# Zero products early on TensorE, half-line offsets for the project operands, and a GpSimd way for weight parts: a float32 attention and MLP kernel on one core

## The chip, the cores and the metric

The kernel runs on one core of a Trainium2 chip. The metric is the device time of one execution in microseconds (us). Engines carry the names of the profile: PE is TensorE (PEld its weight loads), DVE is VectorE, ACT is ScalarE, POOL is GpSimd and SP is SyncE; a q behind a name (PEldq, SPq) marks the engine's instruction queue.

## What is computed

Local attention with a few global keys, and two gated MLPs behind it, all in float32, for 2 batches of 768 positions. Cut to what matters:

```python
scores = scale * q @ k.T + bias            # 8 heads of 64; kept: 96 back, 8 global keys
a = softmax(scores); x = a @ v             # (2, 768, 512)
gate = sigmoid(causal_conv5(x, conv_w))    # first MLP, d_model 512
x = (gate * (x @ w_val)) @ w_out
h = relu(x @ w_in)                         # second MLP, d_ff 1024
out = (h * sigmoid(conv3(h, conv_w2))) @ w_out2
```

The kernel multiplies `w_out` and `w_in` into one matrix W of 512 x 1024 beforehand.

## The kernel before

The 12 tiles of 128 positions (6 per batch) go through attention one by one (`fast_attention`). For each tile PE forms the scores of two halves of 4 heads (L461), DVE adds the bias and takes the row's least value (L472), ACT takes exp and the row sum (L477), DVE inverts the sum and scales (L491, L498), PE transposes (L522), ACT copies the result out of PSUM (L526), and PE multiplies by v (L540). Tile 0 needs only its own keys, which lie in a corner of `x` (`c.first`); every other tile uses its own keys and those of the tile before.

Beside attention the weights are prepared. They arrive as 64-bit numbers in `raw` tiles (`unit`, L291) and become float32 in four steps (`to_f32`): ACT scales (L262), POOL prepares the remainder (L264), DVE joins the bits (L269, L272). The products of the MLPs take each operand as a rounded part (high) and a remainder (low), and `mm3` (L243 to L245) adds three products: high by high, high by low, low by high. `split_ops` makes the two parts: ACT the high (L234), DVE the low (L236). For `w_val` (4 units of 128 x 512, tiles `wvh`, `wvl`) and `w_out2` (8 units, tiles of the pool `w8`), `parts_unit` makes an `m` tile and splits it. W itself is 32 float32 products of 512 columns (L319, `weights`), whose results are split too (`Wh`, `Wl`).

The MLPs run over 4 chunks (2 batches, each of 400 and 368 positions). `values` multiplies by `w_val`, `hidden` by W (operands `gg`), `gated` does the second convolution and gate and splits the result into `g2`, and `project` multiplies `g2` by `w_out2`: for each chunk 3 groups of 128 positions, 8 blocks of 128 of the 1024 columns, 3 products each, 512 columns wide. In the last chunk one group is cut into two of 256. In `project` the parts of `g2` (pool `late`) are what PE loads as weights, and those of `w_out2` (pool `w8`) stream past them. In the profile `g2` and the `w8` tiles are named `g` and `w`, and PSUM tiles `s`, `t`, `x` and `f`.

The order on each engine is made by a planner (class `Plan`). Each piece of work has a list of engines with an assumed cost, its buffers, and what it reads and writes; `lay` goes through time and gives each engine the waiting piece of highest rank, and a piece that has several ways goes to the engine on which it would end first by these costs. So one changed cost or way can move instructions anywhere behind it. Only the first instructions (L834 to L844) stand by hand: the loads of the first tile, the positions, and two loads of a number into a register on every engine (L841), on which a branch depends (L938).

The SBUF pools lie behind each other in the order in which they are opened (`const`, `w8`, `wst`, `sg`, then `at` during attention, whose place `late` takes over). All start at a multiple of 64 bytes.

Of the kernel before, what the change touches and what calls it, by code (L numbers as in the profile page):

```python
# [9 lines left out]
F32 = mybir.dt.float32  # L10
F32R = mybir.dt.float32r
I32 = mybir.dt.int32
AF = mybir.ActivationFunctionType
ALU = mybir.AluOpType
AX = mybir.AxisListType
PSUM = bass.MemoryType.PSUM

P = 128
# [192 lines left out]
def act_us(n, sbuf=True, scaled=False, sums=False):  # L211
    return 0.05 + 0.000834 * n + 0.042 * sbuf + 0.092 * scaled + 0.093 * sums


def dve_us(n, scaled=False):
    return 0.069 + 0.001042 * n + 0.061 * scaled
# [6 lines left out]
def pool_us(n):  # L223
    return 0.17 + 0.0013 * n


def dma_us(kb):
    return max(0.4, kb / 385.0)


def split_ops(c, hi, lo, src, n, bufs, reads, writes, sbuf=True):

    nc, pl = c.nc, c.plan
    pl.add("ACT", act_us(n, sbuf), lambda: nc.scalar.activation(hi(), src(), AF.Copy), bufs, reads, [writes + ("hi",)])  # L234
    pl.add(
        "DVE", dve_us(n), lambda: nc.vector.tensor_tensor(lo(), src(), hi().bitcast(F32), ALU.subtract),  # L236
        bufs, reads + [writes + ("hi",)], [writes + ("lo",)],
    )


# [47 lines left out]
def unit(c, dst, src, a, col, bufs, token, e=None):  # L288

    nc, raw = c.nc, c.raws.new()  # L290
    dma = lambda: nc.sync.dma_start(raw.t.rearrange("p d t -> p (d t)"), rows(src, a, col))  # L291
    c.plan.add("SP", dma_us(512), dma, [raw], [], [("raw", raw)], delay=LANDING)
    view = (lambda: raw.t) if e is None else (lambda: raw.t.rearrange("p (e x) t -> p e x t", e=e))
    to_f32(c, dst, view, 512, [raw] + bufs, [("raw", raw)], token)


def weights(c):
# [35 lines left out]
    for a in range(4):  # L333
        parts_unit(c, c.w_val, a, lambda z, a=a: c.wv[z][:, a, :], [], ("wv", a))


def parts_unit(c, src, a, part, bufs, token):
    m = c.ms.new()
    unit(c, lambda: m.t, src, a, 0, [m], token + ("m",))
    split_ops(c, lambda: part(0), lambda: part(1), lambda: m.t, 512, [m] + bufs, [token + ("m",)], token)  # L340


def second_weights(c):
    c.wo2 = [[c.w8.new() for _ in "hl"] for _ in range(2)]
    for a in range(8):
        two = c.wo2[a // 4]
        parts_unit(c, c.w_out2, a, lambda z, a=a, two=two: two[z].t[:, a % 4, :], two, ("wo2", a))


def scratch(c):  # L350

    x = [c.x[:, d, XP:] for d in range(NC1)]
    c.rel, c.w, c.d = (x[d][:, 0:WIN] for d in range(3))
    c.key, c.far, c.d0 = (x[d][:, 4 * P : 5 * P] for d in range(3))


def positions(c):

    nc = c.nc
    nc.gpsimd.iota(c.rel, pattern=[[-1, WIN]], base=P, channel_multiplier=1, allow_small_or_imprecise_dtypes=True)  # L360
    nc.gpsimd.iota(c.key, pattern=[[1, P]], base=0, channel_multiplier=0, allow_small_or_imprecise_dtypes=True)
    nc.gpsimd.affine_select(
        out=c.rel, in_=c.rel, compare_op=ALU.is_ge, fill=BIG, base=P, pattern=[[-1, WIN]], channel_multiplier=1
    )
# [44 lines left out]
def fast_attention(c, ap):  # L409

    nc, ident, pl = c.nc, c.ident, c.plan
# [9 lines left out]
    kq, vs = {}, {}  # L421

    def keys(t, pr, what):
        return c.first[0][:, pr, what] if t == 0 else kq[t].t[:, pr, what]
# [4 lines left out]
    def load(t):  # L429
        b, i = tiles[t]  # L430
        if t == 0:
            return
        kq[t], vs[t] = kqr.new(), vr.new()
        pl.add("SP", dma_us(512), lambda: nc.sync.dma_start(kq[t].t, c.kq[b, i]), [kq[t]], [], [("kq", t)], delay=LANDING)
        src = c.v[b, i * P : (i + 1) * P].rearrange("s h d -> s (h d)")
        pl.add(
            "SP", dma_us(256), lambda: nc.sync.dma_start(vs[t].t.rearrange("p a h d -> p (a h d)"), src),
            [vs[t]], [], [("v", t)], delay=LANDING,
        )

    def held(d, ts):
        return [d[t] for t in ts if t in d]

    for t in range(nt):
# [3 lines left out]
        js = [t - 1, t] if i else [t]  # L448
        nk = len(js) * P
        st, p = sts.new(), {}  # L450
        load(t)
        for half in range(2):
            s = [c.ring["s"].new() for z in range(2)]

            def scores(half=half, s=s, js=js, t0=t):
                for pr in (2 * half, 2 * half + 1):
                    for n, j in enumerate(js):
                        for z in range(2):
                            hs = slice(z * D, (z + 1) * D)
                            out = s[z].t.rearrange("p (a w) -> p a w", w=WIN)[:, pr % 2, n * P : (n + 1) * P]  # L460
                            nc.tensor.matmul(out, keys(t0, pr, 1)[hs], keys(j, pr, 0)[hs], start=True, stop=True)  # L461

            pl.add(
                "PE", 0.43 * len(js), scores, s + held(kq, js), [("kq", j) for j in js], [("s", t, half)], mode="s"
            )
            for h in range(4 * half, 4 * half + 4):
                p[h] = pr_.new()

                def least(h=h, s=s, st=st, w=p[h], nk=nk, i=i):
                    sc = s[h % 2].t.rearrange("p (a w) -> p a w", w=WIN)[:, h // 2 % 2, :nk]  # L470
                    bias = c.B[:, h, :] if i else c.B0[h]
                    nc.vector.tensor_tensor_reduce(  # L472
                        w.t[:, :nk], sc, bias, -QKSCALE, 3.0e38, ALU.add, ALU.min, st.t[:, 0, h : h + 1]
                    )

                def grow(h=h, st=st, w=p[h], nk=nk):
                    nc.scalar.activation(  # L477
                        w.t[:, :nk], w.t[:, :nk], AF.Exp, bias=st.t[:, 0, h : h + 1], scale=-1.0,
                        accum_out=st.t[:, 1, h : h + 1],
                    )  # L480

                bias = ("B" if i else "B0", h)
                pl.add("DVE", dve_us(nk), least, [p[h], s[h % 2], st], [("s", t, half), bias], [("p", t, h)])
                pl.add("ACT", act_us(nk, True, True, True), grow, [p[h], st], [], [("p", t, h)])
            hs = slice(4 * half, 4 * half + 4)

            def guard(st=st, hs=hs):
                nc.gpsimd.tensor_scalar(st.t[:, 1, hs], st.t[:, 1, hs], 1.0e-9, 1.0, ALU.add, ALU.mult)

            def invert(st=st, hs=hs):  # L490
                nc.vector.reciprocal(st.t[:, 2, hs], st.t[:, 1, hs])  # L491

            four = [("p", t, h) for h in range(4 * half, 4 * half + 4)]
            pl.add("POOL", 0.12, guard, [st], four, [("r", t, half)])
            pl.add("DVE", 0.2, invert, [st], [], [("r", t, half)])
            for h in range(4 * half, 4 * half + 4):
                def on_dve(h=h, st=st, w=p[h], nk=nk):
                    nc.vector.tensor_scalar(w.t[:, :nk], w.t[:, :nk], st.t[:, 2, h : h + 1], None, ALU.mult)  # L498

                pl.add("DVE", 0.13 + 0.00052 * nk, on_dve, [p[h], st], [("r", t, half)], [("p", t, h)])  # L500
# [312 lines left out]
def attention_gated_mlps(ctx, tc, kq, v, nn, w_val, conv_w, w_out, w_in2, w_out2, out):  # L813
    nc = tc.nc
    c = Ctx()
# [4 lines left out]
    c.const = ctx.enter_context(tc.tile_pool(name="const", bufs=1))  # L820
    w8 = ctx.enter_context(tc.tile_pool(name="w8", bufs=1))
    c.wst = ctx.enter_context(tc.tile_pool(name="wst", bufs=1))
    sg = ctx.enter_context(tc.tile_pool(name="sg", bufs=1))
    c.small = ctx.enter_context(tc.tile_pool(name="small", bufs=1, side="right"))
    c.x = c.const.tile([P, NC1, XW], F32, name="x")
# [7 lines left out]
    with tc.manual_schedule():  # L833
        nc.sync.dma_start(c.li.rearrange("p n t -> p (n t)"), c.nn.to_broadcast([P, 4]))  # L834
        nc.scalar.dma_start(k0[:, 0:2], kq[0, 0, :, 0:2])
        nc.sync.dma_start(k0[:, 2:4], kq[0, 0, :, 2:4])
        nc.scalar.dma_start(v0, v[0, 0:P].rearrange("s (a h) d -> s a h d", a=4))
        scratch(c)
        positions(c)
        nc.vector.memset(one, 0.0)  # L840
        _, (glo, ghi, llo, lhi) = nc.values_load_multi_w_load_instructions(c.nn)  # L841
        nc.scalar.activation(one, one, AF.Exp)
        nc.gpsimd.memset(c.x[:, :, 0:XP], 0.0)
        make_identity(nc, c.ident)  # L844
        first_mask(c)
# [9 lines left out]
    def arm(fast):  # L855
        with ExitStack() as es:
# [4 lines left out]
            pl = c.plan = Plan()  # L861
            ap = pools.enter_context(tc.tile_pool(name="at", bufs=1)) if fast else None
            late = {}

            def late_pool():
                if not late:
                    pools.close()
                    late["p"] = pools.enter_context(tc.tile_pool(name="late", bufs=1, reuse_waits="tile"))
                return late["p"]

            def all_keys(b):
# [110 lines left out]
```

## Time and profile before

| | |
|---|---|
| median of 3 runs | 289.07 us (288.51 to 289.23) |
| profiled execution, its own time | 288.96 us |
| its span in the profile | 287.2 us |
| PE busy | 269.2 us, 94% of the span |
| DVE busy | 238.6 us, 83% |
| ACT busy | 192.6 us, 67% |
| POOL busy | 68.5 us, 24% |

The span runs from the first to the last instruction; the rest of the execution's time, 1.8 us, lies around it. Busy time of PE counts overlapping matmuls once, and a matmul is shown longer than the time it keeps the next one waiting, so the distance from one start to the next is what a matmul costs in a row of them.

### The profile page before, as it was taken

The numbers are of one execution on the slowest core, as the hardware profiler recorded it, in microseconds if no ns is written. First come the engines' busy times: TensorE is split into PE (matmuls) and PEld (weight loads), VectorE is DVE, ScalarE is ACT, GpSimd is POOL, SyncE is SP. The second block draws the span as 40 slices with busy tenths as digits, with TensorE's granted clock in tenths as the row PEclk, the third lists the DMA queues.
The fourth block names the chain that finished last, engine by engine and source line by source line (L and its number), as shares of the span: only waits on it lengthen the run. The fifth ranks groups of instructions, "written<-read, shape, count | busy, mean of one in ns | idle before, by whom it ended". The sixth has DMA issues, their size and how long they took to land.

```text
span 287.2 us, 5402 instructions
## 1 busy us (share of the span) xinstructions
PE 269.2 (94%) x1832; PEld 228.0 (79%) x1832; DVE 238.6 (83%) x637; ACT 192.6 (67%) x486; POOL 68.5 (24%) x160
## 2 busy tenths in 40 slices
PE   2687899899999999999999999999999999999993
PEld 2565666565447999999999999988999988899882
DVE  3999999999999999999899999999986654357600
ACT  2899998988568989988778544875355354454510
POOL 4422223522111120212353512360612000003000
PEclk9999999999999999999999999999999999999999
DMA  4984668637406301004510000010000011000112
GB/s 132 362 312 168 188 216 266 237 102 266 149 2 219 102 19 49 10 2 155 181 40 0 2 0 1 1 39 37 38 2 0 0 73 39 37 0 2 40 73 84
DMA packets 10277, 26.18 MB, mean 91 GB/s; under 512 B 1408, under 2 KB 2688, under 8 KB 10240
## 3 DMA queue, kind: packets, MB, share of 16 engines
q1 hardware_dynamic: 9440, 25.22, 26.3%
q10 hardware_dynamic: 800, 0.52, 0.6%
q8 instruction: 16, 0.26, 0.4%
q14 instruction: 21, 0.17, 0.2%
HBM read 22.59 MB, written 3.15 MB: 90 GB/s over the span
## 4 chain that ended last, share of the span: by engine, by line
PE 72%; DVE 20%; issue 3%; DMA 2%; ACT 1%; POOL 1%; SPq 0%; DVEq 0%; POOLq 0%
PE s L244 8%; PE s L245 8%; PE s L243 8%; PE f L243 7%; PE f L245 7%; PE f L244 7%; DVE p L472 5%; DVE p L498 4%; PE s L461 4%; PE x L540 4%; PE t L522 4%; DVE raw L269 3%; PE t L243 2%; PE x L245 2%; PE t L245 2%
## 5 line engine op out<-in xcount | busy, mean ns | idle before, releaser
L652 DVE SCALAR_TENSOR_TENSOR z<-h,cw,z 128x384 f32<-128x384 f32 x64 | 40.6, 643 | 12.6 <-ACT z L647 10.9
L477 ACT ACTIVATE p<-p,st 128x256 f32<-128x256 f32 (+1 forms) x96 | 46.0, 482 | 5.8 <-DVE st L472 5.5
L654 ACT ACTIVATE z<-z 128x384 f32<-128x384 f32 (+2 forms) x48 | 25.0, 523 | 26.7 <-DVE z L652 26.4
L244 PE MATMUL s<-w,g 128*128 128x512 f32 (+1 forms) x104 | 39.2, 377 | 0.0
L245 PE MATMUL s<-w,g 128*128 128x512 f32 (+1 forms) x104 | 39.2, 377 | 0.0
L243 PE MATMUL s<-w,g 128*128 128x512 f32 (+1 forms) x104 | 39.1, 376 | 0.0
L652 DVE SCALAR_TENSOR_TENSOR z<-x,cw,z 128x400 f32<-128x400 f32 (+1 forms) x64 | 38.4, 628 | 0.1
L522 PE MATMUL t<-ident,p 128*128 128x128 f32 x176 | 28.6, 281 | 4.7 <-ACT pts L526 4.7
L498 DVE TENSOR_SCALAR p<-p,st 128x256 f32<-128x256 f32 (+1 forms) x96 | 31.1, 368 | 0.7
L522 PEld LDWEIGHTS t<-ident,p 128*128 128x128 f32 x176 | 19.9, 140 | 14.6 <-ACT pts L526 8.5
L472 DVE CUSTOM_DVE_ANT_0 p<-s,B 128x256 f32<-128x256 f32 x80 | 30.7, 417 | 0.4 <-PE t L522 0.4
L319 PE MATMUL f<-w,w 128*128 128x512 f32 x64 | 30.1, 601 | 0.7 <-DVE Wl L236 0.6
L526 ACT ACTIVATE pts<-t 128x512 f32<-128x512 f32 (+1 forms) x48 | 26.5, 553 | 2.5 <-PE t L522 2.1
L243 PE MATMUL f<-gg,Wh 128*128 128x400 f32 (+1 forms) x80 | 27.7, 346 | 0.0
L245 PE MATMUL f<-gg,Wl 128*128 128x400 f32 (+1 forms) x80 | 27.0, 338 | 0.0
L244 PE MATMUL f<-gg,Wh 128*128 128x400 f32 (+1 forms) x80 | 27.0, 338 | 0.0
L461 PE MATMUL s<-kq 64*128 64x128 f32 x320 | 25.0, 291 | 0.5 <-DVE st L472 0.5
L461 PEld LDWEIGHTS s<-kq 64*128 64x128 f32 x320 | 21.0, 194 | 5.5 <-issue 3.2
L264 POOL TENSOR_SCALAR raw<-raw 128x512 f32<-128x512 f32 x24 | 17.7, 739 | 27.2 <-ACT m L262 21.6
L648 POOL TENSOR_SCALAR z<-h,cw 128x384 f32<-128x384 f32 x12 | 11.4, 947 | 49.1 <-DVE z L652 31.0
L245 PEld LDWEIGHTS s<-w,g 128*128 128x128 f32 x104 | 19.5, 188 | 3.8
L236 DVE TENSOR_TENSOR g<-z,g 128x384 fp32r<-128x384 f32 x32 | 17.4, 550 | 5.9 <-ACT g L234 5.9
(114 smaller groups left out, 606.4 us busy)
## 6 DMA issues: line engine op xcount, KB each, us to landing
raw<-in_moe_w_out_dram SPq DMA_DIRECT2D x12, 512.0 KB, 3.4
kq<-in_kq_dram SPq DMA_DIRECT2D x11, 512.0 KB, 5.1
raw<-in_moe_w_in_dram SPq DMA_DIRECT2D x8, 512.0 KB, 4.4
v<-in_v_dram SPq DMA_DIRECT2D x11, 256.0 KB, 3.9
out_dram<-o SPq DMA_DIRECT2D x11, 256.0 KB, 2.0
raw<-in_moe_w_val_dram SPq DMA_DIRECT2D x4, 512.0 KB, 4.0
v<-in_v_dram SPq DMA_DIRECT2D x8, 64.0 KB, 2.7
x<-in_kq_dram ACTq DMA_DIRECT2D x1, 256.0 KB, 4.1
```

What stands on the lines that cost most here:

```text
L243: nc.tensor.matmul(out, lh, rh, start=first, stop=False)
L244: nc.tensor.matmul(out, lh, rl, start=False, stop=False)
L245: nc.tensor.matmul(out, ll, rh, start=False, stop=last)
L319: nc.tensor.matmul(ps.t, big["wot"].t.bitcast(F32)[:, e, cs], big[wi].t.bitcast(F32)[:, e, :], start=e == 0, stop=e == 3)
L461: nc.tensor.matmul(out, keys(t0, pr, 1)[hs], keys(j, pr, 0)[hs], start=True, stop=True)
L472: nc.vector.tensor_tensor_reduce(w.t[:, :nk], sc, bias, -QKSCALE, 3.0e38, ALU.add, ALU.min, st.t[:, 0, h : h + 1])
L477: nc.scalar.activation(w.t[:, :nk], w.t[:, :nk], AF.Exp, bias=st.t[:, 0, h : h + 1], scale=-1.0, accum_out=st.t[:, 1, h : h + 1],)
L498: nc.vector.tensor_scalar(w.t[:, :nk], w.t[:, :nk], st.t[:, 2, h : h + 1], None, ALU.mult)
L522: nc.tensor.transpose(o[:, z, n, :], p[2 * pr + z].t[:, n * P : (n + 1) * P], ident)
L526: nc.scalar.activation(w.t[:, :, :nw, :], o[:, :, :nw, :], AF.Copy)
L652: nc.vector.scalar_tensor_tensor(z(), src(k), w()[:, k : k + 1], z(), ALU.mult, ALU.add)
L654: pl.add("ACT", act_us(n), lambda: nc.scalar.activation(z(), z(), AF.Tanh, scale=0.5), bufs, [], [token])
```

## The change

Three things. **Zero products**: the new function `idle` multiplies zeros by zeros in float32. Three such products (512, 512 and 256 columns, into a PSUM tile that is given back at once) stand by hand right behind the first loads, ahead of PE's register loads. Two more of 512 columns go into the plan between the scores of tile 0 and those of tile 1. **Half a line**: an unused tile of 8 float32 (32 bytes) is put at the head of the pools `w8`, `wst` and `late`. With it all tiles of `w8` and of `late` (the `w_out2` parts, `g2`, and the staging tiles of W's product) begin 32 bytes past a multiple of 64; the pools between are moved by 64 bytes. **GpSimd ways**: `split_ops` takes `pool=True` from `parts_unit` and then gives the high and the low part of `w_val` and `w_out2` a second way on POOL.

```diff
-def split_ops(c, hi, lo, src, n, bufs, reads, writes, sbuf=True):
+def split_ops(c, hi, lo, src, n, bufs, reads, writes, sbuf=True, pool=False):
     nc, pl = c.nc, c.plan
-    pl.add("ACT", act_us(n, sbuf), lambda: nc.scalar.activation(hi(), src(), AF.Copy), bufs, reads, [writes + ("hi",)])
+    more = [
+        {"POOL": (0.1 + pool_us(n), lambda: nc.gpsimd.tensor_scalar(hi(), src(), 1.0, 1.0, ALU.mult, ALU.mult))},
+        {"POOL": (0.6 + pool_us(n), lambda: nc.gpsimd.tensor_tensor(lo(), src(), hi().bitcast(F32), ALU.subtract))},
+    ] if pool else [{}, {}]
+    pl.add(
+        "ACT", act_us(n, sbuf), lambda: nc.scalar.activation(hi(), src(), AF.Copy), bufs, reads, [writes + ("hi",)], **more[0]
+    )
     pl.add(
         "DVE", dve_us(n), lambda: nc.vector.tensor_tensor(lo(), src(), hi().bitcast(F32), ALU.subtract),
-        bufs, reads + [writes + ("hi",)], [writes + ("lo",)],
+        bufs, reads + [writes + ("hi",)], [writes + ("lo",)], **more[1],
     )
...
-    split_ops(c, lambda: part(0), lambda: part(1), lambda: m.t, 512, [m] + bufs, [token + ("m",)], token)
+    split_ops(c, lambda: part(0), lambda: part(1), lambda: m.t, 512, [m] + bufs, [token + ("m",)], token, pool=True)
...
+def idle(c, out, widths):
+
+    for n in widths:
+        zeros = [c.nc.const_aps.tensor(0.0, [P, w], F32) for w in (P, n)]
+        c.nc.tensor.matmul(out[:, :n], *zeros, start=True, stop=True)
...
         load(t)
+        if t == 1:
+            rest = c.ring["f"].new()
+            pl.add("PE", 1.72, lambda rest=rest: idle(c, rest.t, [512, 512]), [rest], [("s", 0, half) for half in range(2)], ["idle"])
...
-                "PE", 0.43 * len(js), scores, s + held(kq, js), [("kq", j) for j in js], [("s", t, half)], mode="s"
+                "PE", 0.43 * len(js), scores, s + held(kq, js), [("kq", j) for j in js] + ["idle"] * (t == 1), [("s", t, half)], mode="s"
...
+    for pool in (w8, c.wst):
+        pool.tile([P, 8], F32, name="half_line")
...
+        with tc.tile_pool(name="pw", bufs=1, space=PSUM) as pw:
+            idle(c, pw.tile([P, 512], F32, name="idle"), [512, 512, 256])
...
                     late["p"] = pools.enter_context(tc.tile_pool(name="late", bufs=1, reuse_waits="tile"))
+                    late["p"].tile([P, 8], F32, name="half_line")
```

How the order changes at the two places of which the prediction speaks. First PE from its first instruction to the scores of tile 1 (`s<-x` are tile 0's scores, `s<-x,kq` and `s<-kq` tile 1's; TENSOR_LOAD to COMPARE_AND_BRANCH are the register loads and the branch). Before:

```order
L841 TENSOR_LOAD in_n_dram_ptr
L841 TENSOR_LOAD in_n_dram
L938 ISA
L938 REGISTER_ALU x3
L938 COMPARE_AND_BRANCH
L461 MATMUL s<-x 128x128 x8
L461 MATMUL s<-x,kq 128x128 x2
L461 MATMUL s<-kq 128x128 x2
```

With the change:

```order
L360 MATMUL idle<-const-float32-0.0 128x512 x2
L360 MATMUL idle<-const-float32-0.0 128x256
L861 TENSOR_LOAD in_n_dram_ptr
L861 TENSOR_LOAD in_n_dram
L959 ISA
L959 REGISTER_ALU x3
L959 COMPARE_AND_BRANCH
L477 MATMUL s<-x 128x128 x8
L360 MATMUL f<-const-float32-0.0 128x512 x2
L477 MATMUL s<-x,kq 128x128 x2
L477 MATMUL s<-kq 128x128 x2
```

The three zero products stand ahead of the register loads, the two others between the scores of tile 0 and tile 1.

Second POOL where the last units of `w_val` are prepared (`raw` rows are L264's step of `to_f32`, L270 with the change; `st` and `kq` rows belong to attention, `z` rows to the first convolution). Before:

```order
L264 TENSOR_SCALAR raw<-raw 128x512 x2
L488 TENSOR_SCALAR st<-st 128x4
L505 TENSOR_SCALAR kq<-gl 128x4x32
L264 TENSOR_SCALAR raw<-raw 128x512
L488 TENSOR_SCALAR st<-st 128x4
L505 TENSOR_SCALAR kq<-gl 128x4x32
L488 TENSOR_SCALAR st<-st 128x4
L648 TENSOR_SCALAR z<-x,cw 128x368
```

With the change:

```order
L236 TENSOR_TENSOR wvl<-m,wvh 128x512
L270 TENSOR_SCALAR raw<-raw 128x512 x2
L521 TENSOR_SCALAR kq<-gl 128x4x32
L236 TENSOR_TENSOR wvl<-m,wvh 128x512 x2
L504 TENSOR_SCALAR st<-st 128x4
L270 TENSOR_SCALAR raw<-raw 128x512
L504 TENSOR_SCALAR st<-st 128x4
L270 TENSOR_SCALAR raw<-raw 128x512
L236 TENSOR_TENSOR w_1479<-m,w_1478 128x512
L521 TENSOR_SCALAR kq<-gl 128x4x32
L664 TENSOR_SCALAR z<-x,cw 128x368
```

Three of the four low parts of `w_val` and the first of `w_out2` now stand on POOL. Over the whole program the planner puts 8 of the 12 low parts (3 of `w_val`, 5 of `w_out2`) and one of the 12 high parts there; in exchange 4 of the 20 first steps of a convolution (`z`) that POOL had go to ACT.

## Rows read from the trace of the kernel before

**Rows 1.** The page: busy time by engine

```profile
PE 269.2 (94%) x1832; PEld 228.0 (79%) x1832; DVE 238.6 (83%) x637; ACT 192.6 (67%) x486; POOL 68.5 (24%) x160
```

**Rows 2.** Windows: stretch, length, busy us (instructions) by engine, granted clock, DMA

```profile
8.00:40.00 32.00, 26.81 (x279) 20.95 (x280) 30.89 (x129) 30.35 (x101) 9.76 (x25) 1.00 0.74 255
40.00:140.00 100.00, 98.06 (x771) 75.45 (x770) 97.35 (x294) 82.92 (x225) 24.45 (x53) 1.00 0.39 123
140.00:282.00 142.00, 142.00 (x770) 129.81 (x768) 106.74 (x196) 76.51 (x156) 31.08 (x68) 1.00 0.08 29
```

**Rows 3.** Waits of PE, 9 to 140 us: total, times, longest

```profile
PE t L522 <- ACT pts L526: 4.7, 7, 1.0
PE s L461 <- DVE x L401: 2.0, 1, 2.0
PE f L319 <- DVE Wl L236: 0.6, 2, 0.4
```

**Rows 4.** Timeline of 0 to 16 us: start, length, what [idle before, releaser]

```profile
4.94 1.81 PEld L461 LDWEIGHTS s<-x 64*128 64x128 f32 x16 [4.94 <-issue]
...
6.66 0.28 DVE L472 CUSTOM_DVE_ANT_0 p<-s,b 128x128 f32<-128x128 f32 x1
...
9.08 0.80 PE L461 MATMUL s<-x,kq 64*128 64x128 f32 x4 [2.03 <-DVE x L401]
...
13.28 0.42 DVE L472 CUSTOM_DVE_ANT_0 p<-s,B 128x256 f32<-128x256 f32 x1 [0.38 <-PE t L522]
...
14.08 1.16 PE L461 MATMUL s<-kq 64*128 64x128 f32 x16
```

**Rows 5.** Single lines: duration ns min/median/max, first and last start us

```profile
L461 PE MATMUL s<-x,kq x16: 417/417/579, 9.1 to 12.0; 64*128 64x128 f32 x16
L461 PE MATMUL s<-kq x144: 272/272/373, 14.1 to 54.9; 64*128 64x128 f32 x144
L841 PEldq TENSOR_LOAD <-in_n_dram_ptr x1: 957/957/957, 0.8 to 0.8; - x1
L841 PEldq TENSOR_LOAD <-in_n_dram x1: 2080/2080/2080, 1.8 to 1.8; - x1
L522 PEldq EVENT_SEMAPHORE  x2: 51/51/51, 10.5 to 10.7; - x2
```

**Rows 6.** The chain that ended last, 4 to 30 us: start, length, what

```profile
9.10 3.77 PE s L461 x32
```

**Rows 7.** Timeline of PE: products of L319, and the end of project

```profile
80.75 5.42 PE L319 MATMUL f<-w,w 128*128 128x512 f32 x12 [0.35 <-DVE Wl L236]
...
269.83 0.40 PE L244 MATMUL s<-w,g 128*128 128x512 f32 x1
...
272.16 0.40 PE L245 MATMUL s<-w,g 128*128 128x512 f32 x1
...
280.02 0.28 PE L243 MATMUL s<-w,g 128*128 128x256 f32 x1
...
281.94 0.28 PE L245 MATMUL s<-w,g 128*128 128x256 f32 x1
```

**Rows 8.** Groups by line and shape: xcount | busy us, mean ns

```profile
L243 PE MATMUL s<-w,g 128*128 128x512 f32 x88 | 34.7, 394 | 0.0
...
L243 PE MATMUL s<-w,g 128*128 128x256 f32 x16 | 4.4, 278 | 0.0
...
L236 DVE TENSOR_TENSOR wvl<-m,wvh 128x512 fp32r<-128x512 f32 x4 | 2.7, 692 | 0.0
```

**Rows 9.** Single lines, as in rows 5: later products, POOL, a DVE operation

```profile
L540 PE MATMUL x<-pts,v x112: 272/273/324, 23.9 to 54.3; 128*64 128x128 f32 x112
L522 PE MATMUL t<-ident,p x82: 272/273/331, 13.7 to 58.8; 128*128 128x128 f32 x82
L264 POOL TENSOR_SCALAR raw<-raw x24: 647/673/1055, 13.3 to 160.9; 128x512 f32<-128x512 f32 x24
L498 DVE TENSOR_SCALAR p<-p,st x61: 273/348/758, 39.9 to 128.1; 128x256 f32<-128x256 f32 x53, 128x128 f32<-128x128 f32 x8
```

## The prediction

> **What bounds the kernel now.** First the page [rows 1]: PE is busy for 94% of the span, no other engine above 83%. An average says little, so the windows come next [rows 2]. From 140 us on PE has no gap (142.00 of 142), from 40 to 140 it lacks 1.94 us. From 8 to 40 us it lacks 5.2 us, while DVE (30.89 of 32) and ACT (30.35) are full: there the softmax work sets the pace. So time can be won in three ways only: DVE or ACT earlier or freer before 40 us, one of the few waits of PE after that, or a shorter step of the products themselves. The list of PE's waits [rows 3] names what there is to win in the first two: 4.7 us for `pts`, 2.0 us once for the keys of tile 1 (`x`), 0.6 us for the low parts of W. After its last product at 281.94 [rows 7] PE leaves some 5 us of copying and storing to the span of 287.2, which no part of the change touches.
>
> Then the clock. The windows print a granted clock of 1.00, but the scores show two levels [rows 4, 5]: those of tile 1 last 417 ns at 9.1 to 12.0 us, those from 14.1 us on 272 ns. Sixteen of the later ones take 1.16 us [rows 4], so (1.16 - 0.27) / 15 = 0.059 each; the 32 of tile 1 take 3.77 us in the chain [rows 6]. That is 1.2 GHz before and 2.4 GHz after. Ahead of the change PE had been idle to 4.97, had worked for 1.8 us, and was idle for 2.03 us more.
>
> **Part 1, the zero products.** The three early ones (two of 512 columns, one of 256) are 5 halves of a product. A record of L319 is half of a float32 product of 512 columns, and twelve take 5.42 us [rows 7], 0.44 each at 2.4 GHz (0.43 with the last one's long end taken off), so 0.86 a product there and 1.72 at 1.2 GHz. The three take 2.5 x 1.72 = 4.3 us, and can begin where PE's register loads begin now, at 0.8 us [rows 5]. They end at 5.1 to 5.2 us, 0.2 us past the first weight load at 4.94. That 0.2 us is covered: DVE takes the first of tile 0's scores only at 6.66 [rows 4], 1.7 us behind their start, and without that cover it would cost just the 0.2 us. The register loads and the branch behind the products stand on PE's queue, which runs ahead of the array: the semaphores of L522 pass at 10.5 and 10.7 us [rows 5], while scores that stand ahead of them start until 12.0. So I count the loads (0.8 to 3.9 us, then the branch) as running beside the zeros. The bound the other way: they begin only when the zeros end, 5.1 + 4.1 = 9.2, so the first scores are 4.3 us late.
>
> The two later products stand in the gap of 2.03 us. At 2.4 GHz they last 1.72 us and fit; at 1.2 GHz 3.4 us, which would end 1.4 us past the start of tile 1's scores at 9.08. Behind them on PE's queue stand just these scores. PE then has worked almost without a break from 0.8 us; before, the higher level came after work from 9.08 on, so I expect it ahead of tile 1. That takes 3.77 - (31 x 0.059 + 0.27) = 1.65 us off its scores. Not all of this moves the end: DVE is still occupied with tile 0. It idles for 0.38 us at 13.28, waiting for PE [rows 4], and for 1.1 us in all of 8 to 40 [rows 2]. Between these I take **-0.8**; the ends are -1.65 (the scores alone bound) and +4.3 (above).
>
> **Part 2, half a line.** It changes no instruction in `project`, only where its operands lie. PE is full there, so each nanosecond of a product counts: 3 x 88 = 264 products of 512 columns and 3 x 16 = 48 of 256 [rows 8]. Their steps are (272.16 - 269.83) / 10 = 0.233 and (281.94 - 280.02) / 17 = 0.113 us [rows 7]. Columns alone, one a cycle at 2.4 GHz, would be 0.213 and 0.107; L319's passes of 512 columns take 0.219. So a product has an excess of 0.014 to 0.020 us, 264 x 0.020 + 48 x 0.006 = 5.6 us in all at most. Does it come from the place of the operands? The nearest rows are the products by v (L540), whose operands lie 32 bytes past a multiple of 64, and the transposes (L522), which lie on one: 272 and 272 ns [rows 9]. They are of 128 columns and of another number format, so they only lean. I take **0**, and keep -5.6 (all excess gone) and +2.8 (half as much again) as ends. The pools between move by 64 bytes, which leaves them on multiples of 64. The two unused tiles are no instruction.
>
> **Part 3, low parts on POOL.** Eight of 12 lows leave DVE: 8 x 0.692 = 5.5 us [rows 8]. On POOL a step of this size with one operand lasts 0.673 [rows 9]; a low has two, so 0.67 to 1.4 (twice the row of DVE) each, 11 us at most, and POOL is 76% idle [rows 1]. One high and the four `z` steps between POOL and ACT go together: ACT has 17 us free in 40 to 140 [rows 2], so 0. Most of the relief lies where PE never waits and is worth nothing. What PE can win are its waits: the two for `Wl` are 0.6 us [rows 3], because the lows of `w_val` stand on DVE between those of W; with them all gaps from 40 to 140 would be 1.94 [rows 2]. Behind a slower low nobody waits at once: the products by `w_val` come later. I take **-0.6**; ends -1.9 and +0.7 (one low late by a whole operation). What is late next is ACT's `pts`. No DMA is added; SP issues the same loads, some of them one to three places earlier or later, and the DMA engines are 74% busy from 8 to 40 us and 39% after that [rows 2], so I count that as 0.
>
> POOL beside DVE may slow DVE: L498 lasts 273 at the least, 348 in the middle, 758 ns at the most [rows 9]. If each of eight lows cost DVE 758 - 348 = 0.41 us, 3.3 of the 5.5 us would be lost, still a gain for DVE. The Trainium skill goes further: "Perfetto Trace Analysis", section "Optimizing Scalar/DVE Operations", says that GpSimd and DVE share a read port of SBUF, so moving work between them might not help. By that rule this part would be 0 and the time 288.2; the row of L498 agrees that something stretches DVE, not that it takes everything.
>
> For the price on POOL the Trainium skill's "GPSIMD Engine Reference", section "4.1 Engine selection", has a two-operand operation at 1.96 times the time of DVE; by that a low would be an estimated 1.36 us, near my upper end, and the sum stays.
>
> **Sum.** The profiled execution took 288.96 us (1.8 around a span of 287.2), 0.11 under the median shown. 288.96 - 0.8 + 0 - 0.6 = **287.6**.
>
> **Rivals.**
> - **A, as summed**: 287.6, its own range 286.5 to 288.4. Chance 0.45.
> - **B, the place of operands matters and half a line frees the stream.** Half of the excess gone is -2.8: 284.8; a quarter gives 286.2, all 282.0. For it: the steps stay above the columns' time in the last us too [rows 7], so other engines seem not to be the cause, and something of the operands is left. Against: [rows 9]. Chance 0.34.
> - **C, slower: the same place costs.** If an operand that begins in mid-line makes each row fetch longer, the excess grows by half: +2.8, 290.4. It decides from (1.4 + 0.87) / 312 = 7.3 ns a product on, where parts 1 and 3 are given back and 0.87 more. For it: all operands of `project` are moved off multiples of 64, on which they lie now. Against: [rows 9] again. Chance 0.09.
> - **D, nothing comes through**: tile 1 is still slow, or DVE loses beside POOL what it is spared, or the planner's new order puts new waits of PE in place of the old: 289.0 (288.4 to 289.6). For it: 4.7 us of waits for `pts` [rows 3] show that ACT's order, which also shifts, is tight. Chance 0.09.
> - **E, the zeros hold the register loads**: up to 291.9. Against: the queue that runs ahead [rows 5]. Chance 0.03.
>
> **How the numbers follow.** About 0.3%, 0.87 us, can be told from no change: 288.2 to 289.9. Faster: A but for 0.05, and B, 0.74. Same: 0.05 of A and D, 0.14. Slower: C and E, 0.12. The range from 282.8 to 289.6 takes in A, D and B but for its far end, and leaves out C, E and some 0.06 of B.
>
> **What would show it.** Part 1: scores of tile 1 at 272 ns, the first of tile 0 still near 5.2 us, no idle time of DVE near 13 us; wrong if they stay at 417 or start past 6 us. Part 2: starts in `project` 0.233 apart as before (A), 0.213 to 0.228 (B) or over 0.240 (C). Part 3: no wait of PE for `Wl`, lows on POOL of 0.7 to 1.4 us, L498's middle not much over 348 ns; wrong if PE's waits between 40 and 140 us sum to 1.9 or more. The forecast falls if `project` moves by more than 4 ns a product: 312 of them are 1.2 us, more than either other term.

## The result and the profile after

The changed kernel takes 292.12 us (median of 6 runs, 291.73 to 293.08), the kernel before on the same chip 289.08 (6 runs, 288.51 to 289.90). The ratio is 1.0103 with a 95% interval of 1.0085 to 1.0121: slower by 3.0 us, where 287.6 was forecast and the range ended at 289.6. The profiled execution took 292.29 us, its span is 290.4.

The page of the changed kernel begins with the busy time by engine; [rows 1] are the answer to it before.

```profile
PE 275.7 (95%) x1842; PEld 228.4 (79%) x1842; DVE 241.4 (83%) x629; ACT 192.6 (66%) x487; POOL 73.9 (25%) x167
```

DVE has 8 instructions fewer and is busy 2.8 us longer (241.4 against 238.6). That is the first sign: eight low parts (lows) left it, 5.5 us of work, and its time grew. PE's extra 6.5 us are about the 6.6 us of the zero products.

The windows of the changed kernel, columns as in [rows 2]:

```profile
8.00:40.00 32.00, 27.84 (x325) 21.66 (x325) 31.60 (x140) 31.26 (x105) 9.40 (x24) 1.00 0.78 263
40.00:140.00 100.00, 96.47 (x724) 72.10 (x721) 97.60 (x279) 79.64 (x217) 34.48 (x60) 1.00 0.37 121
140.00:285.00 145.00, 143.84 (x774) 130.57 (x773) 108.69 (x194) 78.98 (x160) 26.55 (x68) 1.00 0.08 28
```

Before 40 us PE does more than it did (325 matmuls against 279). Behind 40 us it now lacks 3.53 us up to 140 and 1.16 after that, where it lacked 1.94 and nothing. The waits of PE from 9 to 285 us name the new gaps:

```profile
PE t L538 <- ACT pts L542: 4.8, 7, 1.3
PE t L538 <- DVE p L514: 2.0, 1, 2.0
PE s L251 <- DVE g L242: 0.8, 1, 0.8
```

The wait for `pts` is as large as before [rows 3], that for `Wl` is gone. New are 2.0 us for `p` and 0.8 us for `g`, both DVE's.

**Where DVE is late.** The timeline of POOL, and then that of DVE, around the wait of 2.0 us (start, length, what):

```profile
87.93 1.49 POOL L236 TENSOR_TENSOR wvl<-m,wvh 128x512 fp32r<-128x512 f32 x1 [3.32 <-ACT wvh L239]
90.71 1.28 POOL L236 TENSOR_TENSOR wvl<-m,wvh 128x512 fp32r<-128x512 f32 x1 [1.29 <-ACT wvh L239]
```

```profile
88.20 1.77 DVE L278 SCALAR_TENSOR_TENSOR m<-m,raw 128x512 int32<-128x512 int32 x1
...
90.16 0.68 DVE L242 TENSOR_TENSOR Wl<-f,Wh 128x512 fp32r<-128x512 f32 x1
90.76 1.38 DVE L514 TENSOR_SCALAR p<-p,st 128x256 f32<-128x256 f32 x1
```

Both times DVE's instruction begins just behind a low on POOL and ends only behind POOL's end: 88.20 + 1.77 = 89.97 against 87.93 + 1.49 = 89.42 on POOL, and 92.14 against 91.99. L278 on `m` has a median of 0.68 us and took 1.77; L514 has 0.35 and took 1.38. On PE the transposes that need this `p` start late:

```profile
92.29 0.63 PE L538 MATMUL t<-ident,p 128*128 128x128 f32 x4 [1.97 <-DVE p L514]
```

The same view by line, for all of the program (duration ns min/median/max, first and last start us):

```profile
L236 POOL TENSOR_TENSOR w<-m,w x5: 1387/1483/2002, 102.8 to 173.2; 128x512 fp32r<-128x512 f32 x5
L236 POOL TENSOR_TENSOR wvl<-m,wvh x3: 1281/1492/1561, 76.3 to 90.7; 128x512 fp32r<-128x512 f32 x3
L278 DVE SCALAR_TENSOR_TENSOR m<-m,raw x12: 677/682/1770, 74.0 to 171.8; 128x512 int32<-128x512 int32 x12
L514 DVE TENSOR_SCALAR p<-p,st x96: 269/348/1381, 10.0 to 131.2; 128x256 f32<-128x256 f32 x80, 128x128 f32<-128x128 f32 x16
```

Beside each of the eight lows the trace has one DVE instruction that is stretched by 0.4 to 1.1 us over its group's median, and in one place a second, by 0.3, which began ahead of the low beside another POOL step; in all these are 8.0 us. The lows left DVE 8 x 0.692 = 5.5 us lighter [rows 8]. The balance, 2.5 us more, is close to the 2.8 by which DVE's busy time grew. No instruction waits for a low itself in this trace.

**The other two parts.** Tile 1's scores and two pieces of `project` in the changed kernel (first the view by line, then PE's timeline):

```profile
L477 PE MATMUL s<-x,kq x16: 272/272/373, 9.0 to 10.6; 64*128 64x128 f32 x16
```

```profile
270.47 0.39 PE L249 MATMUL s<-w,g 128*128 128x512 f32 x1
...
272.10 0.40 PE L250 MATMUL s<-w,g 128*128 128x512 f32 x1
...
283.00 0.28 PE L251 MATMUL s<-w,g 128*128 128x256 f32 x1
...
285.16 0.28 PE L251 MATMUL s<-w,g 128*128 128x256 f32 x1
```

Tile 1's scores last 272 ns, where they lasted 417 [rows 5]. Of `project` the step of 512 columns is (272.10 - 270.47) / 7 = 0.233, as before [rows 7]; that of 256 is (285.16 - 283.00) / 18 = 0.120 and was 0.113, which is 48 x 0.007 = 0.3 us.

### The profile page after: what moved, and what is told of

It is laid out like the page before. It is cut to its first block, busy times and chain, and to the rows that moved or that the text cites. A ratio compares the mean times of both kernels' runs of the same rounds, so it can differ in the third digit from the quotient of the medians.

```text
span 290.4 us, 5425 instructions
## 1 busy us (share of the span) xinstructions
PE 275.7 (95%) x1842; PEld 228.4 (79%) x1842; DVE 241.4 (83%) x629; ACT 192.6 (66%) x487; POOL 73.9 (25%) x167
## 4 chain that ended last, share of the span: by engine, by line
DVE 45%; PE 37%; issue 5%; ACT 5%; DMA 4%; POOL 2%; DVEq 0%; POOLq 0%; ACTq 0%
DVE z L668 13%; DVE p L514 6%; PE s L249 6%; PE s L250 6%; PE s L251 6%; DVE p L488 6%; DVE m L278 3%; DVE raw L275 3%; PE f L249 3%; PE f L250 3%; PE f L251 3%; DVE g L242 2%; ACT p L493 2%; PE x L556 2%; DVE z L781 2%
## 5 line engine op out<-in xcount | busy, mean ns | idle before, releaser
L668 DVE SCALAR_TENSOR_TENSOR z<-h,cw,z 128x384 f32<-128x384 f32 x64 | 39.7, 629 | 13.2 <-ACT z L663 11.6
L668 DVE SCALAR_TENSOR_TENSOR z<-x,cw,z 128x400 f32<-128x400 f32 (+1 forms) x64 | 41.0, 676 | 0.0
L514 DVE TENSOR_SCALAR p<-p,st 128x256 f32<-128x256 f32 (+1 forms) x96 | 31.9, 372 | 0.7
L325 PE MATMUL f<-w,w 128*128 128x512 f32 x64 | 30.7, 599 | 0.0
L270 POOL TENSOR_SCALAR raw<-raw 128x512 f32<-128x512 f32 x24 | 18.5, 770 | 28.5 <-ACT w L268 14.2
L477 PEld LDWEIGHTS s<-kq 64*128 64x128 f32 x320 | 20.4, 187 | 5.5 <-issue 3.2
L251 PEld LDWEIGHTS s<-w,g 128*128 128x128 f32 x104 | 19.6, 188 | 5.1 <-DVE g L242 1.2
L242 DVE TENSOR_TENSOR g<-z,g 128x384 fp32r<-128x384 f32 x32 | 18.3, 582 | 5.9 <-ACT g L239 5.9
L249 PEld LDWEIGHTS s<-w,g 128*128 128x128 f32 x104 | 19.6, 188 | 4.0 <-ACT g L239 0.7
```

Source lines behind the costliest of these rows:

```text
L249: nc.tensor.matmul(out, lh, rh, start=first, stop=False)
L251: nc.tensor.matmul(out, ll, rh, start=False, stop=last)
L325: nc.tensor.matmul(ps.t, big["wot"].t.bitcast(F32)[:, e, cs], big[wi].t.bitcast(F32)[:, e, :], start=e == 0, stop=e == 3)
L668: nc.vector.scalar_tensor_tensor(z(), src(k), w()[:, k : k + 1], z(), ALU.mult, ALU.add)
```

## The experiments

Theory H: a low on POOL reads two operands and holds the DVE instruction beside it until POOL is done; PE's new waits come from that. Rivals: the planner's new order (O), the half line (S), the zero products (Z). Ratios below are to the kernel before, timed on the same chip, with the 95% interval.

**1. The lows back on DVE, in the same order.**

```diff
-{"POOL": (0.6 + pool_us(n), lambda: nc.gpsimd.tensor_tensor(lo(), src(), hi().bitcast(F32), ALU.subtract))},
+{"POOL": (0.6 + pool_us(n), lambda: nc.vector.tensor_tensor(lo(), src(), hi().bitcast(F32), ALU.subtract))},
```

> The changed kernel (292.1 us) with its order kept, but each low part that stands on POOL is computed by the same subtraction on DVE, at the same place of the order. Theory H (hold): a low on POOL holds up the DVE instruction beside it until POOL is done; the eight hold DVE for 8.0 us and spare it 5.5, and PE's new waits come from this. Then DVE has no instruction over 1.1 us between 75 and 180 us, PE's waits for p (L514, 2.0 us) and g go, and the time is 288.0 to 289.5. Rival O (order): the loss comes from the planner's new order of the work, whichever engine computes; then PE's waits stay and it is 291.5 to 293.

Measured: 290.25 us, ratio 1.0025 (1.0006 to 1.0044). PE, ACT and SP have the very same order as in the changed kernel. The wait for `p` falls from 2.0 to 0.4 us and that for `g` from 0.8 to 0.4. DVE has no instruction over 1.01 us between 75 and 180 us, as H said. So 1.9 us by the medians, 2.3 by the ratios, hang on the engine of the lows, and O falls as the main cause; but the time is 0.7 us above H's end. A likely reason, argued and not shown by itself: the planner's order counts on a lighter DVE, and here DVE carries the 5.5 us again. (5), the same order with a lighter DVE, fits it.

**2. Without the way on POOL at all** (`pool=True` taken out of `parts_unit`).

> The changed kernel without the second way on POOL (zero products and half line stay). H: the loss goes, and what the zero products gain early stays: 287.5 to 288.8. Rival S (half line): the cost lies in the moved operands; then it stays near 291 to 292.

Measured: 291.42 us, ratio 1.0060 (1.0035 to 1.0084). H missed. The time lies in S's range, but (3) and (6) show that the half line does not cost this. The planner lays another order here: two transposes of tile 0 stand on PE behind the zero products, ahead of tile 1's scores, which start at 11.73 us and not at 9.08 as before. PE's timeline, and the window of the stretch behind it (columns as in [rows 2]):

```profile
10.48 0.41 PE L538 MATMUL t<-ident,p 128*128 128x128 f32 x2 [2.12 <-DVE p L514]
```

```profile
11.60:15.10 3.50, 3.50 (x33) 3.37 (x32) 2.96 (x11) 1.31 (x5) 0.67 (x2) 0.51 1.00 341
```

After the gap of 2.12 us the granted clock is 0.51 for 3.5 us, and in this stretch lie tile 1's scores. The higher clock that the zero products brought was gone behind the gap. So nothing of part 1 is seen in this order, and the runs of this kernel spread from 289.94 to 292.02.

**3. Without the half line** (the two `half_line` edits taken out).

> The changed kernel without the unused tiles of 32 bytes. H: within 0.4 us of 292.1, since only the 48 products of 256 columns have a longer step with half a line (0.120 against 0.114 us, 0.3 us in all). Rival S: 289 to 290, the operands' place is what costs.

Measured: 292.70 us, ratio 1.0106 (1.0062 to 1.0150), which can't be told from the changed kernel's 1.0103. The median of four runs is 0.2 us above H's end; S falls.

**4. Without the zero products** (both calls of `idle` and the plan's entry taken out).

> The changed kernel without the five zero products. H with the clock's gain kept apart: tile 1's scores are back at 417 ns, and the time is 292.5 to 293.5, as the zeros give about 0.9 us before 60 us. Rival Z: the zeros cost, because the first scores start 0.5 us later with them; then it is 291 to 291.8.

Measured: 295.47 us, ratio 1.0195 (1.0135 to 1.0255), slower than H's upper end by 2.0. Z falls, but the size is not that of the zeros alone, since the planner lays a third order with six lows on POOL. Tile 1's scores are at 417 ns, as H said, but as in (2) transposes of tile 0 stand ahead of them, and they start at 12.08 us, 3.0 later than before. PE has a gap of 2.06 us in it at 191 us, in `project`, and the clock falls behind it. The timeline of PE there, and the window:

```profile
193.30 0.50 PE L249 MATMUL s<-w,g 128*128 128x512 f32 x1 [2.06 <-ACT o L813]
...
194.35 0.63 PE L249 MATMUL s<-w,g 128*128 128x512 f32 x1
...
196.48 0.63 PE L251 MATMUL s<-w,g 128*128 128x512 f32 x1
```

```profile
193.80:197.20 3.40, 3.40 (x9) 2.63 (x9) 3.37 (x7) 3.07 (x7) 0.78 (x1) 0.50 0.26 84
```

PE works without a break in those 3.4 us and gets half of the clock: a gap costs its own length and another 1.7 us here, half of the 3.4.

**5. The low on POOL with one operand**, all orders kept. It leaves out the subtraction.

```diff
-lambda: nc.gpsimd.tensor_tensor(lo(), src(), hi().bitcast(F32), ALU.subtract)
+lambda: nc.gpsimd.tensor_scalar(lo(), src(), 1.0, 1.0, ALU.mult, ALU.mult)
```

> The changed kernel (292.1 us) with its order kept, but the eight low parts on POOL are a copy of one operand (a step as L270's, 0.65 to 0.9 us) in place of the subtraction of two (1.3 to 2.0 us); the low parts are left out by this. Theory H (hold): the DVE instruction beside POOL's step is held as long as that step lasts; DVE loses some 8 x 0.4 = 3 us in place of 8.0, and the time is 290 to 291. Rival O (order): 291.7 to 292.7, as only the place of the step counts.

Measured: 288.02 us, ratio 0.9950 (0.9924 to 0.9976): 4.1 us below the changed kernel and faster than the kernel before. O falls. H's number was too high by 2 us, for a reason that is not shown. The lines of POOL, by line and around the place of above, then the two DVE instructions of above, then PE:

```profile
L236 POOL TENSOR_SCALAR w<-m x5: 864/923/1397, 99.7 to 167.5; 128x512 fp32r<-128x512 f32 x5
L236 POOL TENSOR_SCALAR wvl<-m x3: 660/892/940, 76.0 to 88.7; 128x512 fp32r<-128x512 f32 x3
```

```profile
86.63 0.94 POOL L236 TENSOR_SCALAR wvl<-m 128x512 fp32r<-128x512 f32 x1 [2.65 <-DVE m L278]
88.68 0.66 POOL L236 TENSOR_SCALAR wvl<-m 128x512 fp32r<-128x512 f32 x1 [1.11 <-DVE m L278]
```

```profile
87.92 0.68 DVE L278 SCALAR_TENSOR_TENSOR m<-m,raw 128x512 int32<-128x512 int32 x1
...
89.38 0.34 DVE L514 TENSOR_SCALAR p<-p,st 128x256 f32<-128x256 f32 x1
```

```profile
89.86 0.63 PE L538 MATMUL t<-ident,p 128*128 128x128 f32 x4
```

L278 and L514 have their usual 0.68 and 0.34 us, and PE's transposes start without a wait. But no POOL step lies beside these two any more: a copy is shorter, and it waits for `m` alone, where a low waited for ACT's high part too, so it starts earlier. The hold itself is still there: six of the eight copies stretch one DVE instruction each, by 0.34 to 0.41 us, and counted as above the sum is 2.4 us in place of 8.0 (H: some 3). DVE's busy time is 235.7 us in place of 241.4. So the run shows what eight subtractions cost against eight copies, and not the price of the hold alone.

PE's order is the same in four of these kernels, so one can follow when the same PE instruction starts in each (us):

| PE instruction | one operand (5) | val one operand (9) | on DVE (1) | the change | change less (5) |
|---|---|---|---|---|---|
| x by v, before any low | 63.13 | 63.85 | 63.63 | 63.40 | 0.3 |
| x by v, behind `w_val`'s lows | 91.02 | 91.70 | 92.33 | 93.44 | 2.4 |
| scores, behind the low at 102.8 | 104.22 | 105.59 | 106.27 | 107.31 | 3.1 |
| project, behind the low at 149.5 | 150.24 | 152.89 | 152.70 | 154.63 | 4.4 |
| last project product | 280.38 | 283.46 | 282.85 | 285.16 | 4.8 |

The last column jumps in three places, each behind a low: by 1.8 us at the transposes of 92.29, by 0.7 at the scores behind the low of 102.8, and by 1.3 in `project` at 153 to 155 us. The rest is small: 0.3 ahead of all lows, 0.3 at 81 us and 0.4 at 191 us. Behind the low at 134 us and those at 167 and 173 the column stays as it is: PE does not wait there.

**6. The half line alone** on the kernel before, whose order stays.

> The kernel before with the unused tiles of 32 bytes alone, its order unchanged. Theory: project's steps of 512 columns stay at 0.233 us and those of 256 go from 0.114 to 0.120: 0 to 0.5 us above the kernel before. Rival S: the place of the operands matters by a microsecond or more, in either direction.

Measured: 289.36 us, ratio 0.9992 (0.9974 to 1.0010). The steps are as expected, 0.233 us for 512 columns and 0.120 for 256, where before has 0.114; the 0.3 us that this makes in all can't be seen in the time. S falls for good.

**7. The zero products alone, in the order of before.** The three early ones as in the change; the two others are issued from `scores` and not planned:

```diff
+                if t0 == 1 and half == 0:
+                    idle(c, c.ring["f"].make(), [512, 512])
```

> The kernel before with the five zero products at the same places, but outside the plan: no other engine's order of computation changes, no part goes to POOL, no half line. Theory W (warm): the higher clock ahead of tile 1 is worth what the sum said, and only the planner's new order spoiled it without POOL; tile 1's scores last 272 ns, and the time is 0.5 to 1.2 us below the kernel before. Rival N: DVE sets the pace up to 40 us, so that tile 1's faster scores change nothing: within 0.4 us of before.

Measured: 288.41 us, ratio 0.9958 (0.9939 to 0.9977). W holds. It has the lowest time of the versions with all of the computation in them, though (8), (10) and (11) can't be told from it. Only one load of `v` is issued two places earlier on SP. Its line for tile 1's scores, and PE's timeline a little later:

```profile
L470 PE MATMUL s<-x,kq x16: 272/272/374, 9.0 to 10.5; 64*128 64x128 f32 x16
```

```profile
12.91 0.44 PE L531 MATMUL t<-ident,p 128*128 128x128 f32 x2 [1.54 <-ACT pts L535]
```

PE leads the kernel before by 1.86 us at the first transpose behind tile 1's scores (10.94 against 12.80 us), then waits 1.54 us for ACT, and leads by 0.8 us from 14 to 40 us, by 0.55 to 56 us, and by 0.75 at the end (281.19 against 281.94 for the last product).

**8. Only the three early products, in the order of before.**

> The kernel before with the three early zero products alone, its order of computation unchanged; the gap of 2 us ahead of tile 1 is open. Theory G (gap): the clock rises before 8 us, and the gap of 2 us takes it down again for some 3.4 us, as after gaps of 2.0 to 2.1 us in three other runs; most of tile 1's scores last 417 ns, and the time is within 0.4 us of the kernel before. Rival: the early products are enough, tile 1 runs at 272 ns, and the time is 0.5 to 1.2 us lower.

Measured: 288.67 us, ratio 0.9977 (0.9956 to 0.9997). G is wrong on tile 1: its scores ran at 272 ns, behind a gap of 2.53 us, and by the medians the time is 0.8 us below the kernel before, as the rival said. In the profiled run the clock fell later, behind the next gap of 1.67 us; the window of that stretch:

```profile
13.80:17.20 3.40, 3.40 (x28) 2.52 (x26) 3.26 (x13) 3.40 (x14) 0.74 (x2) 0.50 1.00 389
```

**9. One operand for `w_val`'s lows alone**; the five of `w_out2` stay a subtraction, and the order stays. It leaves out the subtraction of `w_val`.

> The changed kernel with its order kept; the three low parts of w_val on POOL are a one-operand copy (the subtraction is left out there), the five of w_out2 stay the two-operand subtraction. H with sizes from the two traces: against the version in which all eight are one-operand (288.0 us), PE's lag in the changed kernel grows by 2.4 us from 75 to 100 us, where the three of w_val lie, and by 1.9 after that. So with w_val's taken out: 289.5 to 290.3. Rival (slack): one long hold at 90.8 us, in front of a transpose, makes the loss, the later ones are absorbed: 287.8 to 288.6.

Measured: 290.35 us, ratio 1.0030 (1.0012 to 1.0049), just over H's end. Of the table above, the lag to (5) grows by 0.7 us ahead of all lows, where the kernels do not differ, stays there behind `w_val`'s lows, and grows by 0.7 us to the scores of 104 us and by 1.3 to `project` at 150 us, behind the lows of `w_out2` that are left. The rival, that only the one long hold counts, falls.

**10. A shorter start: 512, 512 and 128 columns early**, otherwise as 7.

> The kernel before in its order with zero products of 512, 512 and 128 columns early and the two of 512 ahead of tile 1. With 256 columns as the third the early ones ended at 5.4 us and the first scores started at 5.49, 0.5 us later than before. Theory L (late start): this one ends 0.4 us earlier, the scores start at 5.0 to 5.1, the higher clock is still there for tile 1, and the time is 1.2 to 1.7 us below before (0.5 less than with 256). Rival: the first scores wait for nothing that matters and DVE takes them no sooner; then it is within 0.2 us of the one with 256, some 1.0 to 1.2 below before.

Measured: 288.62 us, ratio 0.9969 (0.9954 to 0.9985); 0.4 us below the kernel before by the medians and 0.9 by the ratio; L missed. The first scores start at 5.12 us, about as wanted. In the profiled run the clock was high from 3.9 us, fell behind a gap of 1.54 us and was 0.50 from 14.1 to 17.5 us, which 7 did not have.

**11. Two products early**, otherwise as 7.

> As before, but early only two zero products of 512 columns. L: a free gap of some 0.6 us ahead of the first scores; the scores start at 4.97. If the clock still rises ahead of 9 us, as early as with three, the time is that of the version with 512, 512 and 128; if the rise comes behind the start of tile 1, part of the gain goes: 0.3 to 0.8 us below before.

Measured: 288.57 us, ratio 0.9972 (0.9957 to 0.9987). The clock rose only at 9.8 us, so the two later zero products took 3.16 us in place of 1.99, and tile 1's scores started at 10.47, at the higher clock but late. By the medians 0.5 us of gain is left. Between 7, 10 and 11 the intervals overlap; nothing says that a shorter start helps.

## Why the prediction was wrong

- **Part 3 failed, in the step "if each of eight lows cost DVE 758 - 348 = 0.41 us, 3.3 of the 5.5 us would be lost, still a gain for DVE".** The price was read from the longest L498 beside a POOL step of one operand and 0.67 us. A two-operand low lasts 1.3 to 2.0 us, and DVE's instruction is held to its end: 8.0 us in all, 1.0 for each. With 0.41 no loss for DVE was possible, so part 3 was bounded by +0.7; rival D, which names a DVE that loses what it is spared, went to 289.6. The forecast's own sign came: from 40 to 140 us PE's waits are 3.5 us, where 1.9 was to show it wrong. "Behind a slower low nobody waits at once" was right; what waits is the DVE instruction beside it, and behind that PE, 2.0 us for `p` and 0.8 for `g`.
- **Both numbers were at hand.** The forecast already had the two that make the loss: a low on POOL of up to 1.4 us, and a DVE that is stretched beside POOL. They had to be joined: DVE is held until POOL's instruction ends, so up to 8 x 1.4, not 8 x 0.41. The trace of the kernel before showed this already: its longest L498 starts at 39.87 us, just behind a `raw` step of POOL (39.77 to 40.48), and ends at 40.63, just behind that step. In the end time the eight lows on POOL cost 1.9 us against the same lows on DVE (1), and 4.1 us against the shorter copies (292.12 against 288.02 in 5). That lows on POOL delay PE is so shown; how the whole 3.0 us divide between the hold and the planner's order is not.
- **The relief of part 3, -0.6, is not shown.** PE's wait for `Wl` is gone, as forecast. But the one version with cheap steps on POOL, (5), lies only 0.4 us under (7), its interval overlaps that of (7), and the two orders differ. The price of a low was near the stated 0.67 to 1.4 us: 1.28 to 2.00, median about 1.5. (The Trainium skill's "GPSIMD Engine Reference" has the figure 1.96, which the forecast quotes, in section "3.1 Elementwise — side-by-side cycle accounting"; its section 4.1 has about 2.)
- **Part 1 was right in size and reason**: -0.8 was forecast, and PE leads by 0.55 to 0.82 in (7), 1.0 us by the medians. Behind tile 1's scores the lead was 1.86, of which the scores' shorter steps are 1.7 (the forecast's sum there gives 1.67, not 1.65); PE's wait for ACT took back the rest. The register loads ran beside the zeros, but the scores started at 5.48, 0.5 and not 0.2 us late, since the early products lasted 4.6 us and not 4.3.
- **Part 2 was right**: 0 was forecast, and (3) and (6) show no more than the 0.3 us of the 256-column steps. Rival B, with 0.34, was given too much; rows 9 had spoken against it.
- **C, E and D**: C and E did not come. The slower side came by part 3: D has its mechanism, but at 289.6 at most, as if DVE could lose no more than it was spared.
- **A rule that was at hand.** DVE's instruction that ran freely beside a low is telling: at 90.16 `Wl<-f,Wh` (one operand from PSUM) took its usual 0.68 us. Those that were held are L278, L668 and L242's `gg<-z,gg`, which read two tiles in SBUF, and L514, a scaling of one tile. The Trainium skill, "SBUF — State Buffer", section "Who interferes with whom", says just this: DVE with two SBUF inputs contends with a GpSimd instruction that reads SBUF, and so does DVE in a mode that uses both ports (which `tensor_scalar` can enter); the first to issue has the shared ports for its whole instruction and the other fully blocks. The traces agree (1.77 against 0.68, 1.38 against 0.35); in which mode L514 ran, no run here shows. The weaker rule that the forecast quoted, that such an offload "might not help", gave 288.2 and was too mild as well.

## What to carry to other kernels

Before an elementwise step is moved to GpSimd, take its length there, and count up to that length as DVE's loss for each place where DVE meets it with two SBUF operands or a scaling (here 1.0 us of a low's 1.5, and 0.35 of a copy's 0.9); the relief can be worth it only if that sum is smaller than what DVE sheds. This planner knew only the step's own cost and chose wrongly. It also laid another order when a part was left out, and in (2) and (4) tile 1's scores started 2.7 and 3.0 us late by that, so keep the order fixed when parts are compared. Where PE is full, look for gaps of some 2 us: behind several of them the clock was halved for another 3.4 us.

## What the runs showed besides

- **A gap of PE can cost twice.** Gaps of 2.12 (2), 2.06 (4), 1.95 us (3, at 90.1 us) were each followed within some 2 us of PE's next start by 3.4 us at half of the clock; in the changed kernel's profile a gap of 1.97 us at 90.3 us was not, in (8) one of 1.67 us was and one of 2.53 us was not, and one of 1.54 us was in (10) and was not in (7). So the length alone does not tell, and the cost differs from run to run. This fits the spread of the runs in (2): the five from 291.77 us on have a mean granted clock of 0.986 to 0.987, the five faster ones 0.990 to 0.996, and one stretch of 3.4 us at half of the clock makes about 0.006.
- **The clock's first rise moves too.** In the profiled run of (6), 290.38 us, sixteen scores from 14.48 us on still took 2.08 us, where before they took 1.16 [rows 4], and from 18 us on PE stayed 1.1 to 1.4 us behind the kernel before. The kernel before has runs from 288.3 to 290.9 us. So part of the gain of the zero products in the medians may be that such a late rise is avoided; no trace of a slower run of the kernel before is there to show it.
- **The excess of a product vanishes at the lower clock.** In (4) the products of 512 columns in the slow stretch start (196.48 - 194.35) / 5 = 0.426 us apart, which is 512 columns at 1.2 GHz; at 2.4 GHz they take 0.233, not 0.213. So the 0.020 us over the columns' time is nothing that a product carries at either clock, and for 512 columns it doesn't depend on a shift of 32 bytes. What it is stays open.
- **Half a line costs short products a little.** Products of 256 columns start 0.120 us apart in each trace with the half line and 0.114 in each without it, (3) and the changed kernel included, whose orders are the same. Those of 512 columns show no difference.
